# Moving the first three raw loads of w_out from ahead of V of chunk 1 to behind the reload of chunk 3's K, in a DeltaNet and MLP kernel

## The chip, the cores and the metric

The kernel runs on one core of a Trainium2 chip. The metric is the device time of one execution in microseconds (us). Three runs of the kernel before took 634.31, 634.44 and 635.64 us; their median is 634.44 us. Traces are stretched over one profiled execution, and their times count from its first instruction.

## The reference: what is computed

Two parts follow one another. The first is a DeltaNet recurrence for 4 batches of 8 heads, 768 tokens, 48 values per head:

```python
for t in range(S):
    kt, vt, bt = k_n[:, :, t], v[:, :, t], beta[:, :, t, None]
    y[:, :, t] = einsum('bhd,bhde->bhe', q[:, :, t], state)
    v_old = einsum('bhde,bhd->bhe', state, kt)
    state = state + bt[..., None] * einsum('bhd,bhe->bhde', kt, vt - v_old)
```

Here `k_n` is k divided by its norm. The second part is an MLP on the 3072 tokens of 384 values: `gelu(x @ w_in) @ w_out`, with `w_in` 384 x 2048 and `w_out` 2048 x 384. Both weights come in double precision, everything else in single precision.

## The kernel before, in words

**Tiling.** The 768 tokens are cut into 12 chunks of 64. One unit (`tiles[c, a]`) is chunk c of two batches, side by side on 128 partitions; every chunk has two units. For each chunk the kernel loads K, Q and V, forms products of K with itself and with Q, inverts a triangular system (an elimination of 32 rows on VectorE for the first two pairs of chunks, lines 503 to 529; on GpSimd later), solves for the updates, updates the state, and turns the result into tokens. The MLP of a chunk runs on TensorE beside the recurrence of the chunks that follow. From chunk 2 on, the MLP's products are formed by a scheme with fewer multiplications that needs sums of weights.

**The weights.** [...] There are 16 groups: 0 to 7 are `w_in`, 8 to 15 are `w_out`, two row blocks of `w_out` each. `fetch(n)` (line 206) issues the raw load of group n on SyncE: three DMAs of 256 KB for a group of `w_in`, into space that later holds `w_out` (the trace calls it `w_out_sb`), and two DMAs of 384 KB for a group of `w_out`, into one of three buffers `slots` (the trace calls them `w_raw`). The decoding of group n is `begin(n)` (VectorE, line 235 or 238), `exponents(n)` (ScalarE, line 241), `mantissas(n)` (VectorE, lines 255 and 257) and `signed(n)` (VectorE, line 264 for some groups, and 265). `signed(n)` then calls `fetch(n + 3)` for `w_out`, since its buffer is free: so groups 8, 9 and 10 are loaded by a loop of their own, and 11 to 15 by `signed(8)` to `signed(12)`.

**Order of the work.** The start, up to `by_hand.close()` (line 1260), is written out by hand for all engines. After it, `plan` lists steps with due times in units of a chunk; `emit` (line 1149) writes them in order of these times. In this second part VectorE keeps the written order, while a scheduler orders the other queues. SyncE issues nearly all DMAs, in order: an instruction that waits holds up all behind it. Eight completion semaphores serve its DMAs in turn, and each DMA first waits for the one eight places ahead to land.

**The lines around the change.** By hand, SyncE gets: Q of chunk 2 and K of chunk 3 (two units each), groups 2 and 3 of `w_in`, then groups 8, 9 and 10 of `w_out` (line 1205), then `load_v(1)`, V of chunk 1 (line 1207). V of chunk 1 is scaled on GpSimd (line 385), and read by VectorE in `subtract` (lines 738 and 744). In the plan follow the loads of groups 4 to 7 by `signed(0)` to `signed(3)`, then `load(3)` at 1.06 (line 1281; K and Q of chunk 3, K into its buffers once more), `load_v(2)` at 1.07 (line 1303; V of chunk 2), then the block-wise K of chunk 4 (`load_blocks`, line 138, 16 small DMAs into `Qp`). `begin(8)`, the first step that needs a raw group of `w_out`, is the first of `decode_steps(n_in, NW)`, at 1.365 and later (line 1279).

Of the kernel before, what the change touches and what calls it, by code (L numbers as in the profile page):

```python
# [19 lines left out]
def kernel(  # L20
# [122 lines left out]
    def load_v(c):  # L143
        if c >= NC:
            return
        for a in range(NA):
            u = tiles[c, a]
            u.V = io.tile([128, H, D], F32, tag="V", name="V", bufs=4)
            fetch_in(u.V, v, u)
# [47 lines left out]
    n_in = len(w_parts)  # L197
# [6 lines left out]
    slots = [su.tile([128, 2 * WG], U32, tag=f"w_raw{i}", name="w_raw", bufs=1) for i in range(3)]  # L204

    def fetch(n):
        if n >= len(w_parts):
            return
        dst, src = w_parts[n]
        if n < n_in:  # L210
            raw = stage[:, n % NS * 2 * WG:(n % NS + 1) * 2 * WG]
        else:
            raw = slots[(n - n_in) % len(slots)]
        w_raw[n] = raw.rearrange("q (n w) -> q n w", w=2)
        raw = raw.rearrange("q (m n w) -> q m n w", m=dst.shape[1], w=2)
        for m in range(dst.shape[1]):
            nc.sync.dma_start(out=raw[:, m], in_=src[:, m])
# [480 lines left out]
    def join_steps(g):  # L698
        a, b = range(NA), range(NA, 2 * NA)
        return [(join_run, g, a, ()), (join_run, g, b, a), (join_run, g, (), b)]  # L700
# [232 lines left out]
    def blocks(c):  # L933

        return FH // 2 if c < 4 else FH // 4
# [191 lines left out]
    def ffn_steps(c):  # L1127
        ones = [(1.3, fc1, c, f) for f in range(NF)]
        if c > 1:
            return [(0.88, part_of_layer, c, b, n) for b in range(FH // blocks(c))  # L1130
                    for n in ("P1", "P5", "P6", "P2", "R22", "R11", "P7", "P3", "R12", "P4", "R21")] + [
                (2.6, second_layer, cc, n) for cc in range(c, c + 1 + (c > 3))
                for n in (1, 5, 2, 6, 4, 7, 3)]
        twos = [(2.7, fc2, tiles[c, a], f, f + 4) for a in range(NA) for f in range(0, NF, 4)]
        if c == 0:
            twos.sort(key=lambda s: s[3])
            more_ = [(1.3, fc1, 1, f) for f in range(EARLY)]
            return ones + twos[:-2 * NA] + more_[:4] + twos[-2 * NA:-NA] + more_[4:] + twos[-NA:]
        return ones[EARLY:] + twos

    def at(first, last, steps):

        total, done, timed = sum(s[0] for s in steps), 0.0, []
        for w, *step in steps:
            timed.append((first + (last - first) * (done + 0.5 * w) / total, step))
            done += w
        return timed
# [54 lines left out]
        fetch_in(Qp[2 + a][:, :, 0:D], k, tiles[3, a])  # L1202
    for n in range(2, NS):
        fetch(n)
    for n in range(n_in, n_in + len(slots)):
        fetch(n)
    load_v(1)
    for u in third:
        transposed(u, (0,))
# [60 lines left out]
    def state_at(c, *times, first=(), second=(), last=()):  # L1270

        steps = state_steps(c, first, second, last)
        if len(times) > len(steps):
# [3 lines left out]
    plan = [at(c + 1 + 0.25 * (c == 1), c + 2 + 0.25 * (c == 0), ffn_steps(c)) for c in range(4)]  # L1277
    plan += [at(c + 1, c + 3, ffn_steps(c)) for c in range(4, NC, 2)]
    plan += [decode_in(), at(1.365, 1.9, decode_steps(n_in, NW)), at(1.91, 1.911, [(1.0, late)])]
    rows1, join1 = eliminate_steps(1), join_steps(1)  # L1280
    plan += [at(1.06, 1.065, [(1.0, load, 3)]),
             [(t, (join, 0, range(NA, 2 * NA), level)) for level, t in enumerate((1.085, 1.16))],
]
    sums = [(1.0, sum_of_squares, tiles[3, a], h) for a in range(NA) for h in range(H)]
# [63 lines left out]
    for c in (2, 3, *range(4, NC, 2)):  # L1348
        n = FH // blocks(c)
# [78 lines left out]
```

## Time and profile before

| what | value |
|---|---|
| median of three runs | 634.44 us (634.31 to 635.64) |
| span of the profiled execution | 633.5 us |
| median less span | 0.9 us |
| PE busy | 610.3 us, 96% of the span |
| VectorE (DVE) busy | 428.0 us, 68% |
| ScalarE (ACT) busy | 241.9 us, 38% |
| GpSimd (POOL) busy | 209.5 us, 33% |
| DMA, SyncE's queue | 37.34 MB, 30.7% of 16 engines' span |
| mean granted TensorE clock | 0.982 |
| raw loads of w_out, 16 DMAs of 384 KB | 3.3 to 8.1 us to landing, median 4.5 |

The profiled execution's own time is known by its span alone, 633.5 us from the first instruction to the last; what lies around it is taken as the 0.9 us by which the median of the runs is longer.

How to read it: "PE" is TensorE's matmuls, "PEld" its weight loads, "SPq" SyncE's instructions that issue DMAs. A line such as `L264` is line 264 of the kernel before. The chain of waits goes back from the last instruction, at each step to what released it. A busy share over the whole span is a mean over stages: up to about 137 us VectorE is the fullest engine or as full as TensorE, after that TensorE.

### The profile page before, as it was taken

To read this page: it belongs to the slowest core of one execution; us is meant where nothing else is said; L and a number is where in the kernel's file an instruction comes from. 1 tells how busy PE (TensorE), PEld (TensorE's weight loads), DVE (VectorE), ACT (ScalarE), POOL (GpSimd) and SP (SyncE) were. 2 spreads that over 40 slices of the span, in tenths; PEclk is the share of its full clock that TensorE was granted. 3 is DMA by queue.
4 is the path that set the end of the run, shared out by engine and by line. 5 is a ranking of instruction groups with operands and counts; after the bars stand their busy time and mean duration, and the time that the engine had idled before them with its cause. 6 is when DMAs were issued, how large, how long until landed. Compare 5 with 4: busy or idle time off the path is not lost.

```text
span 633.5 us, 20835 instructions
## 1 busy us (share of the span) xinstructions
PE 610.3 (96%) x8998; PEld 546.6 (86%) x8998; DVE 428.0 (68%) x783; ACT 241.9 (38%) x546; POOL 209.5 (33%) x316
## 2 busy tenths in 40 slices
PE   6769999999999989999999999999999999999997
PEld 5657786777899989998899998899998899988997
DVE  6999989999757586664867654968645955432532
ACT  3576877524541255224451124442034322034200
POOL 4044001000489521698112688112687100000000
PEclk9977999999999998999999999999999999999999
DMA  9894765102444423533123523024121001010011
GB/s 132 178 281 143 145 157 160 26 1 49 71 58 62 80 45 40 90 77 40 14 38 58 111 51 45 9 40 88 30 50 20 10 2 27 2 26 1 0 26 26
DMA packets 158428, 39.71 MB, mean 63 GB/s; under 512 B 150016, under 2 KB 153216, under 8 KB 158336
## 3 DMA queue, kind: packets, MB, share of 16 engines
q1 hardware_dynamic: 155664, 37.34, 30.7%
q10 hardware_dynamic: 2672, 1.03, 0.8%
q8 instruction: 71, 1.16, 0.8%
q14 instruction: 21, 0.17, 0.1%
HBM read 33.62 MB, written 4.72 MB: 61 GB/s over the span
## 4 chain that ended last, share of the span: by engine, by line
PE 77%; DVE 16%; issue 2%; SPq 2%; DMA 2%; ACT 1%; DVEq 0%
PE psX L928 12%; PE psY L994 10%; PE psY L928 8%; PE psX L994 8%; PE psV L994 5%; PE psZ L994 5%; PE psV L928 4%; PE psZ L928 4%; PE psK L727 3%; DVE tmp L523 3%; DVE Nu L525 3%; PE psO L895 3%; PE psG L423 2%; PE psH L877 2%; PE psY L792 2%
## 5 line engine op out<-in xcount | busy, mean ns | idle before, releaser
L360 POOL TENSOR_TENSOR n<-n,half 128x16 f32<-128x16 f32 x10 | 30.0, 3004 | 188.8 <-DVE n L358 139.0
L525 POOL TENSOR_TENSOR Nu<-Nu,tmp 128x30 f32<-128x30 f32 (+14 forms) x120 | 65.3, 544 | 9.0
L523 POOL TENSOR_TENSOR tmp<-Nu 128x30 f32<-128x30 f32 (+14 forms) x120 | 61.3, 510 | 9.3
L994 PE MATMUL psX<-xT,w_in_sb 128*128 128x256 f32 (+1 forms) x288 | 63.2, 350 | 0.0
L928 PE MATMUL psX<-w_out_sb,G 128*128 128x192 f32 x320 | 56.1, 329 | 0.0
L994 PEld LDWEIGHTS psX<-xT,w_in_sb 128*128 128x128 f32 x288 | 48.8, 194 | 5.1
L928 PEld LDWEIGHTS psX<-w_out_sb,G 128*128 128x128 f32 x320 | 52.2, 190 | 0.7
L877 PE MATMUL psH<-xT,w_in_sb 128*128 128x256 f32 x192 | 44.2, 384 | 1.6 <-ACT G L977 1.5
L895 PE MATMUL psO<-w_out_sb,G 128*128 128x384 f32 x128 | 43.9, 490 | 0.0
L877 PEld LDWEIGHTS psH<-xT,w_in_sb 128*128 128x128 f32 x192 | 35.7, 190 | 8.7 <-ACT G L977 2.5
L994 PE MATMUL psY<-xT,w_in_sb 128*128 128x256 f32 (+1 forms) x192 | 42.2, 350 | 0.0
L1022 DVE TENSOR_TENSOR psY<-psY,pu 128x512 f32<-128x512 f32 x20 | 14.0, 700 | 40.4 <-PE psY L994 38.9
L977 ACT COPY xT<-psX 128x768 f32<-128x768 f32 x9 | 7.2, 799 | 86.3 <-PE psX L854 86.3
L977 ACT COPY pu<-psZ 128x512 f32<-128x512 f32 x40 | 23.4, 586 | 37.3 <-PE psZ L994 37.3
L994 PEld LDWEIGHTS psY<-xT,w_in_sb 128*128 128x128 f32 x192 | 33.0, 197 | 3.3
L895 PEld LDWEIGHTS psO<-w_out_sb,G 128*128 128x128 f32 x128 | 23.6, 190 | 14.0
L977 ACT ACTIVATE G<-G 128x512 f32<-128x512 f32 x40 | 25.2, 630 | 19.5 <-DVE G L1030 19.4
L1030 DVE TENSOR_TENSOR G<-psY,pu 128x512 f32<-128x512 f32 x20 | 13.8, 689 | 23.4 <-PE psY L994 23.3
L928 PE MATMUL psZ<-T,pu 128*128 128x192 f32 x160 | 28.3, 329 | 0.1
L977 ACT ACTIVATE G<-psY 128x512 f32<-128x512 f32 x20 | 11.9, 597 | 42.7 <-PE psY L994 42.7
L928 PE MATMUL psY<-T,G 128*128 128x192 f32 x160 | 28.2, 329 | 0.0
L928 PE MATMUL psY<-w_out_sb,G 128*128 128x192 f32 x160 | 28.1, 329 | 0.0
(198 smaller groups left out, 1372.8 us busy)
## 6 DMA issues: line engine op xcount, KB each, us to landing
Kp<-in_k_dram SPq DMA_DIRECT2D x76, 96.0 KB, 3.3
w_out_sb<-in_moe_w_in_dram SPq DMA_DIRECT2D x24, 256.0 KB, 5.4
w_raw<-in_moe_w_out_dram SPq DMA_DIRECT2D x16, 384.0 KB, 4.5
V<-in_v_dram SPq DMA_DIRECT2D x48, 96.0 KB, 3.1
out_dram<-o_sb SPq DMA_DIRECT2D x40, 96.0 KB, 2.2
Qp<-in_k_dram SPq DMA_DIRECT2D x64, 32.0 KB, 2.1
Qp<-in_q_dram SPq DMA_DIRECT2D x64, 32.0 KB, 2.1
Qp<-in_q_dram SPq DMA_DIRECT2D x16, 96.0 KB, 4.3
```

The lines of the kernel that those rows point to most:

```text
L360: nc.gpsimd.tensor_tensor(flat, flat, half, op=ALU.pow)
L423: nc.tensor.matmul(psG[HALF[p], r, i * NP + j, :], lhsT=u.Kt[rows, p, j, :], rhs=(u.Qt if x else u.Kt)[rows, p, j, :], start=True, stop=True)
L523: rows_on.tensor_tensor(tmp, nu[:, j + 1:, j:j + 1].to_broadcast([128, n, j]), nu[:, j:j + 1, 0:j].to_broadcast([128, n, j]), op=ALU.mult)
L525: rows_on.tensor_tensor(nu[:, j + 1:, 0:j], nu[:, j + 1:, 0:j], tmp, op=ALU.add)
L727: nc.tensor.matmul(u.psK[to, x, r, j, :], lhsT=(u.Qt if x else u.Kt)[rows, p, j, :], rhs=St[rows, u.a, p ^ r, j, :], start=True, stop=True)
L877: nc.tensor.matmul(psH, lhsT=w_in_sb[:, f // 2, m, f % 2 * 128:(f % 2 + 1) * 128], rhs=xTs[c][:, m, :], start=(m == 0), stop=(m == NM - 1))
L895: nc.tensor.matmul(u.psO, lhsT=G[:, u.a, f, :], rhs=w_out_sb[:, f, :], start=(f == 0), stop=(f == NF - 1))
L928: nc.tensor.matmul(ps_, lhsT=lhs[:, f, :], rhs=rhs[:, f, :], start=first and f == 0, stop=f == FH - 1, skip_group_check=not first)
L977: i = fn(*args, **kw)
L994: nc.tensor.matmul(ps_[:, i], lhsT=lhs[:, f // 2, f % 2 * 128:(f % 2 + 1) * 128], rhs=rhs, start=first and i == 0, stop=True, skip_group_c ...
L1022: nc.vector.tensor_tensor(L1["Y1"], L1["Y1"], L1["pu"][:, 0], op=ALU.add)
L1030: nc.vector.tensor_tensor(half(1, 1), shaped(L1["Y1"]), shaped(L1["pu"][:, 0]), op=ALU.add)
```

## The change

The loop that loads groups 8, 9 and 10 leaves the part written by hand, where it stood ahead of `load_v(1)`, and becomes three steps of the plan, at 1.1 to 1.25:

```diff
     for n in range(2, NS):
-        fetch(n)
-    for n in range(n_in, n_in + len(slots)):
         fetch(n)
     load_v(1)
...
-    plan += [at(1.06, 1.065, [(1.0, load, 3)]),
+    plan += [at(1.06, 1.065, [(1.0, load, 3)]), at(1.1, 1.25, [(1.0, fetch, n) for n in range(n_in, n_in + len(slots))]),
```

In the order of the built programs, TensorE, VectorE and GpSimd keep all their instructions in the same order. On ScalarE four of the scalings of V of chunks 2 and 3 (line 382) change places with activations of `fc1` (line 883). On SyncE:

| place | before | after |
|---|---|---|
| behind group 3 of w_in | groups 8, 9, 10 (6 DMAs), V of chunk 1 | V of chunk 1 |
| next | groups 4 to 7 of w_in, K and Q of chunk 3, V of chunk 2 | the same |
| next | 16 small loads of K of chunk 4 | groups 8, 9, 10 (6 DMAs), then 5 of the 16 |
| next | group 11 | group 11, 10 of the 16 |
| next | 3 DMAs of another K of chunk 4, group 12 | group 12, the last of the 16 |
| next | V of chunk 3 among groups 13, 14 and 15, the last of that K | V of chunk 3 among groups 13, 14 and 15, then the 4 DMAs of that K |

From there on SyncE's order is the same in both.

## The prediction, made before the changed kernel ran

> **What bounds the kernel now.** The change touches loads between 33 and 104 us, so I first read the chain of waits over that stretch, then the timeline of SyncE's queue, then VectorE's timeline where the moved loads are consumed. The chain (start, length, engine and line):
>
> ```profile
> 82.78 2.79 PE psH L877 x12
> 85.56 0.61 PE psY L792 x32
> 86.17 0.47 PE psY L803 x32
> 86.64 0.47 PE psY L792 x32
> 87.11 0.51 PE psY L803 x31
> ...
> 87.64 0.55 DVE St L808
> 88.19 0.88 DVE w_e L264
> ...
> 135.54 2.05 DVE XM L534
> 137.58 0.14 issue
> 137.72 1.15 PE psJ L618 x32
> ```
>
> From 16 to 66 us the chain is VectorE's for the most part, from 66.04 to 87.62 TensorE's, from 87.64 to 137.6 VectorE's without a break, then TensorE's again. So a late raw group costs nothing before 87.64 as long as VectorE has slack, and its full lateness after. TensorE is no cushion there: its timeline has one idle gap from 92 to 140 us, 0.54 us before L618 at 137.72. SyncE's queue:
>
> ```profile
> 33.80 4.91 SPq L217 DMA_DIRECT2D w_raw<-in_moe_w_out_dram  x6
> 39.04 4.02 SPq L100 DMA_DIRECT2D V<-in_v_dram  x4
> 53.12 8.12 SPq L217 DMA_DIRECT2D w_out_sb<-in_moe_w_in_dram  x9
> ...
> 70.78 2.66 SPq L100 DMA_DIRECT2D V<-in_v_dram  x4
> 73.48 9.74 SPq L138 DMA_DIRECT2D Qp<-in_k_dram  x16
> 83.32 0.87 SPq L217 DMA_DIRECT2D w_raw<-in_moe_w_out_dram  x2
> ```
>
> The reader is to see that the six loads of groups 8 to 10 go out at 33.80 and that V of chunk 1 waits behind them. In the changed queue they follow V of chunk 2, so they start when its last issue ends, 73.4 us. Who needs them is in VectorE's timeline, `begin` of groups 8, 9 and 10 and the two steps behind:
>
> ```profile
> 79.21 0.55 DVE L238 TENSOR_SCALAR w_e<-w_raw 128x768 uint32<-128x768 uint32 x1
> ...
> 81.14 0.56 DVE L238 TENSOR_SCALAR w_e<-w_raw 128x768 uint32<-128x768 uint32 x1
> ...
> 84.94 0.55 DVE L238 TENSOR_SCALAR w_e<-w_raw 128x768 uint32<-128x768 uint32 x1
> 86.73 0.56 DVE L808 TENSOR_TENSOR St<-St,psY 128x384 f32<-128x384 f32 x1 [1.24 <-PE psY L803]
> ```
>
> The bracket is the slack: VectorE stands idle 1.24 us before 86.73, waiting for TensorE.
>
> **What leaves 33 to 48 us.** Six DMAs, 2.36 MB, and 4.91 us of SyncE's queue. V of chunk 1 is issued at about 33.8 instead of 39.04. Does anyone profit? (1) GpSimd scales this V at 49.25 (L385), right behind a memset that runs from 46.99 to 49.17; the four loads landed 7.1 to 7.7 us after their issues, and in the stretches of two us the DMA share is 0.29 from 45.8 to 47.8 and 0.03 after, so V was there before 49.25. The order on GpSimd is fixed and the memset waits for VectorE, so earlier V moves nothing. (2) VectorE itself could run faster with fewer DMAs beside it. The same 60 steps of the elimination run twice, once under this traffic. The view by stretches gives length, PE, PEld, DVE, ACT, POOL busy, clock, DMA share and GB/s:
>
> ```profile
> 16.18:39.04 22.86, 17.76 (x295) 14.87 (x296) 20.86 (x61) 14.48 (x53) 0.00 (x0) 0.97 0.87 214
> 112.57:135.44 22.87, 22.87 (x95) 17.59 (x94) 20.88 (x60) 9.39 (x34) 0.00 (x0) 1.00 0.07 18
> ```
>
> 22.86 us at a DMA share of 0.87, 22.87 at 0.07: traffic costs VectorE nothing. (3) No engine's wait from 30 to 46 us is for these loads. Gain: 0.
>
> **What arrives at 73 us.** The issues need eight places of older DMAs landed. K and Q of chunk 3, issued from 66.67 on with 3.5 to 4.5 us to landing, have landed; V's first two, issued near 70.8 and 71.4, land 4.0 later, by 75.4, in time for the fifth and sixth issue. At the 0.42 us of a median w_raw issue the six go out at 73.5, 73.9, 74.3, 74.8, 75.2 and 75.6. Landing: the later pairs of w_raw, behind a short queue, took 3.6 (at 83.3), 4.9 (at 89.1) and 5.4 us (at 92.9). The DMA share falls from 0.86 to 0.43 at 74.8, so V's backlog is short and I take this band: group 8's second DMA lands between 77.5 and 79.3. A DMA of 0.393 MB takes 0.98 us at the 402 GB/s of the sustained stretch; the first burst landed at steps of about 1.16 us (40.7 to 46.5 for six). Two more DMAs are 2.0 to 2.3 us: group 9 is there between 79.5 and 81.6, group 10 between 81.5 and 83.9. Needed: 79.21, 81.14, 84.94. So `begin(8)` is 0 to 0.1 us late, `begin(9)` 0 to 0.5.
>
> Cover for that: VectorE's 1.24 us. ScalarE holds a second one, since its L241 for group 9 (81.79) stands ahead of the activation that ends at 82.99 and frees the buffer that TensorE writes from 84.1 (the second six of the 12 L877 matmuls at 82.78): 1.1 us. Lateness of 0.5 is hidden; the cost is 0. If the cover is gone, each further us costs one.
>
> [...]
>
> **What stands behind in SyncE's queue.** Five small loads of chunk 4's K, then group 11. Group 11 waits for `signed(8)` (L264 ends at 82.56), so it goes out near 82.6 to 83.4, before 83.32. Then ten of the small loads at 0.45 to 0.61 us each (9.74 us for 16): 4.5 to 6.1 us, so group 12 goes out at 89.1 (its buffer is freed by VectorE at 89.06) to 90.2, before 89.14. It landed after 4.9 us, at about 94.4 for its second DMA, and is needed at 95.23: 0.8 us of cover against 0 to 1.1 us of delay, and the three K loads that competed with it before are gone. Cost 0, bound 0.3. Group 13 has the tighter cover, 93.3 + 5.4 = 98.7 against 99.03, but goes out when its buffer is free at 92.88 as before, with one V load issued ahead of it in both. Groups 14 and 15 likewise. V of chunk 3's last half and the other K of chunk 4 come at 100 to 104 us; ScalarE reads the one at about 115, the other at 148.5. The small loads are read by L408 at 151.87. Nothing there.
>
> ScalarE's exchange of four scalings of 0.25 us with activations, at 113 to 118 us, delays or hastens a TensorE buffer by 0.25 us; its cost lies between -0.1 and 0.2, and I take 0.
>
> **Sum.** 0 + 0 + 0 + 0: the span stays 633.5 us, and with the 0.9 us around it 634.4. I add 0.1 for the small waits at `begin(8)` and `begin(9)`: 634.5 us.
>
> **Rivals.**
>
> *Late groups, slower.* The first burst landed 6.9 to 8.1 us after issue. If the six land like that, since V's short rows clog the engines, group 8 is complete at 73.9 + 8.1 = 82.0, 2.8 us late. VectorE's 6.3 us of work from 79.21 then ends at 88.3, L808 slips by 1.55 and its second by 1.2; ScalarE's L241 for group 9 slips by 2.8, TensorE by 2.8 - 1.1 = 1.7. The end is 1.2 to 1.7 us later: 635.7 to 636.2. It decides from 1.1 us of lateness on. For it: one queue feeds the same 16 engines, and V takes a share of 0.67 to 0.86 at only 117 to 163 GB/s. Against it: at 33.8 six loads of 256 KB were queued ahead, at 73.4 only V's.
>
> *A late group 12 to 15, slower by less.* With 0.61 us for each small load and 4.9 us to landing, group 12 is up to 0.3 us late, and a pair of them 0.6: 634.8 to 635.1.
>
> *Earlier V helps, faster.* At 49.52 VectorE's L255 takes 1.19 us where others take 0.55, and L257 behind it 1.47 for 0.96, while GpSimd runs L385: 1.15 us on the chain. Were L385 held by V's landing, an earlier V would move it off these two: 634.4 - 1.15 = 633.3. Against it: GpSimd shows no wait before L385. [...] No run here shows it moved.
>
> *The change doesn't do what it says.* SyncE's queue as built does hold the six loads behind V of chunk 2, so this is excluded.
>
> **How the numbers follow.** No measurable change 0.68 (this holds 0.10 for the small late groups), late groups 0.22, faster 0.06; the rest, 0.04, is unnamed and I split it evenly. A measurement of this kernel can tell about 0.2%, 1.3 us, from no change. Late groups reach from 635.7 up, faster lies at 633.3 and below. Chances: faster 0.08, same 0.68, slower 0.24. The likeliest case alone spans 633.9 to 635.3. The range leaves out the faster case and the upper part of the slow one: 633.7 to 636.1.
>
> **What would show it.** Right: the six loads issue from 73.4, land by 84; L238 for groups 8 to 10 starts within 0.5 us of 79.2, 81.1 and 84.9; VectorE's idle time before L808 is shorter than 1.24 but above zero; L534 at 135.5. Wrong: a wait of VectorE for `w_raw` of over 1.1 us ahead of 86 us, or any wait for it from 88 to 108 us, which shifts L618 from 137.7 one for one; or L385 on GpSimd ahead of 49 us with L255 at 0.55 us.

## The result and the profile after

In one set of runs side by side the changed kernel took 636.31 us (median of 20, 632.70 to 637.87) and the kernel before 634.33 us (20, 632.54 to 637.22): a ratio of 1.0027, 95% interval 1.0015 to 1.0039. It is slower, by 2.0 us. Two later sets gave ratios of 0.9998 (0.9977 to 1.0019) and 1.0015 (0.9999 to 1.0031). All 43 runs of the changed kernel have a mean of 635.65 us, all 142 of the kernel before that this study holds 634.68: 0.97 us more, with twice the standard error at 0.5 (mine, from the listed times). Set by set the means differ by 1.8, 0.4 and 0.9 us. So it loses about 1 us, 0.15%; whether it is above or below the 0.2% that one set can tell is not settled. The two later sets ran on different chips, so a loss that differs from chip to chip isn't excluded.

The profiled execution has a span of 634.6 us (time 636.27). First the chain of waits (start, length, engine and line), the stretch that the prediction showed of before:

```profile
87.31 0.51 PE psY L803 x31
87.84 0.55 DVE St L808
...
92.19 0.88 DVE w_e L264
93.48 5.84 DMA w_raw<-in_moe_w_out_dram
99.41 0.57 DVE w_e L235
100.00 0.95 ACT w_e L241
...
138.26 1.15 PE psJ L618 x32
```

Before, VectorE carried this chain from 87.64 to 137.6 without a break. Now a raw load of `w_out` stands in it, 93.48 to 99.32, and VectorE's `begin(13)` behind it at 99.41 (before 99.03; half of these 0.38 us are there already at `begin(12)`, 95.44 against 95.23): group 13 has become the thing waited for, if by less than a bracket in the timeline shows. L618 comes at 138.26, 0.54 later than 137.72; the table below shows that the kernel before is as much later itself from one execution to the next. SyncE's queue:

```profile
34.33 4.47 SPq L100 DMA_DIRECT2D V<-in_v_dram  x4
...
70.44 2.67 SPq L100 DMA_DIRECT2D V<-in_v_dram  x4
73.15 3.90 SPq L217 DMA_DIRECT2D w_raw<-in_moe_w_out_dram  x6
77.09 3.93 SPq L138 DMA_DIRECT2D Qp<-in_k_dram  x5
83.43 0.82 SPq L217 DMA_DIRECT2D w_raw<-in_moe_w_out_dram  x2
84.31 5.88 SPq L138 DMA_DIRECT2D Qp<-in_k_dram  x10
90.28 0.87 SPq L217 DMA_DIRECT2D w_raw<-in_moe_w_out_dram  x2
```

V of chunk 1 goes out at 34.33 and the six loads of groups 8 to 10 at 73.15, as forecast. The last two lines are the ten small loads and then group 12, at 90.28; before it went at 89.14. Between the five small loads and group 11 the queue stands idle from 81.02 to 83.43. VectorE's `begin(8)` and `begin(9)`, and the step that waits for TensorE:

```profile
79.40 0.55 DVE L238 TENSOR_SCALAR w_e<-w_raw 128x768 uint32<-128x768 uint32 x1
81.97 0.56 DVE L238 TENSOR_SCALAR w_e<-w_raw 128x768 uint32<-128x768 uint32 x1 [0.56 <-DMA w_raw<-in_moe_w_out_dram]
86.91 0.55 DVE L808 TENSOR_TENSOR St<-St,psY 128x384 f32<-128x384 f32 x1 [0.58 <-PE psY L803]
```

The bracket in the second line is new: VectorE stands idle 0.56 us for group 9. The third line shows where it went: the 1.24 us of idle time before L808 has shrunk to 0.58, and L808 itself is 0.18 late. So far this is the forecast.

### The profile page after: what moved, and what is told of

Its sections match the earlier page's. It is cut to its first block, busy times and chain, and to the rows that moved or that the text cites. A ratio compares the mean times of both kernels' runs of the same rounds, so it can differ in the third digit from the quotient of the medians.

```text
span 634.6 us, 20837 instructions
## 1 busy us (share of the span) xinstructions
PE 611.7 (96%) x8998; PEld 547.4 (86%) x8998; DVE 428.5 (68%) x783; ACT 241.7 (38%) x546; POOL 209.8 (33%) x316
## 4 chain that ended last, share of the span: by engine, by line
PE 78%; DVE 11%; ACT 3%; SPq 3%; issue 2%; DMA 2%; DVEq 0%
PE psX L928 12%; PE psY L994 10%; PE psY L928 8%; PE psX L994 7%; PE psV L994 5%; PE psZ L994 5%; PE psG L423 4%; PE psV L928 4%; PE psZ L928 4%; PE psK L727 3%; PE psO L895 3%; SPq L138 2%; PE psH L877 2%; PE psY L792 2%; PE psU L762 2%
## 5 line engine op out<-in xcount | busy, mean ns | idle before, releaser
L877 PE MATMUL psH<-xT,w_in_sb 128*128 128x256 f32 x192 | 45.5, 393 | 0.3
```

The source lines that it names most:

```text
L877: nc.tensor.matmul(psH, lhsT=w_in_sb[:, f // 2, m, f % 2 * 128:(f % 2 + 1) * 128], rhs=xTs[c][:, m, :], start=(m == 0), stop=(m == NM - 1))
```

## The experiments

**Theories.** A: the loss is VectorE's waits for raw groups of `w_out` between 79 and 110 us. B: it is chance, from TensorE's clock and gaps behind 110 us. C: it comes from the front, from V of chunk 1 going ahead at 34 us or from TensorE's granted clock, which was 0.50 from 38.56 to 59.04 us in the trace of the changed kernel and for 13.65 us between 37.59 and 54.66 in that of before. All runs below are to be read with the table behind them (in edited kernels the decoding lines move: `begin` is L237 and L240 in some, L808 is L810). It gives, for one profiled execution of each kernel, how much later than in the first profile of before VectorE's same instruction starts (its order is the same in all): L534 at 39.14, L307 at 109.33, L408 at 238.14, L808 at 251.28. Beside it stand the waits of VectorE for raw groups of `w_out` that its timeline shows in brackets, added up; how long TensorE's granted clock was 0.50 near 236 us; and the span, all in us.

### The two kernels again

No edit: the kernel before, and the changed kernel.

> The kernel before, unchanged, as a control and for a second profile. Theory A (waits of VectorE for raw groups of w_out between 81 and 106 us make the loss), theory B (the loss is chance: TensorE's half-clock periods and issue gaps after 110 us, which differ from execution to execution), theory C (the loss comes from the front: V of chunk 1 ahead, and TensorE at half clock from 38.6 to 59.1 us): all three give 0.998 to 1.002. Its profile tells which of the differences between the first two traces repeat: A expects no wait of VectorE for w_raw and L307 at 109.3 us, C expects TensorE at half clock for some 13 us of the stretch from 37 to 60.

> The changed kernel once more. A and C: 1.002 to 1.004 again (1.2 to 2.5 us). B: 1.000 to 1.001. In the profile A expects VectorE's L238 for group 9 near 82.0 with a wait of some 0.5 us, L235 for group 13 at 99.3 or later, and L307 at 109.8, 0.5 us behind the kernel before; C expects TensorE at half clock for 20 us between 38 and 60 us.

Measured: `before_again` 634.87 us, ratio 1.0004 (0.9985 to 1.0024); `after_again` 634.09, ratio 0.9998 (0.9977 to 1.0019), but its profiled execution took 640.01 with a span of 638.3. VectorE's timeline of `after_again` shows what one execution can lose:

```profile
83.96 0.56 DVE L238 TENSOR_SCALAR w_e<-w_raw 128x768 uint32<-128x768 uint32 x1 [1.72 <-DMA w_raw<-in_moe_w_out_dram]
88.58 0.56 DVE L808 TENSOR_TENSOR St<-St,psY 128x384 f32<-128x384 f32 x1 [0.27 <-PE psY L803]
...
98.10 0.56 DVE L235 TENSOR_SCALAR w_e<-w_raw 128x768 int32<-128x768 int32 x1 [0.90 <-DMA w_raw<-in_moe_w_out_dram]
109.77 0.56 DVE L238 TENSOR_SCALAR w_e<-w_raw 128x768 uint32<-128x768 uint32 x1 [2.19 <-DMA w_raw<-in_moe_w_out_dram]
```

Groups 9, 12 and 15 are waited for, 5.2 us in all with group 8; the cover before L808 is nearly used up (0.27), and L307 is 5.1 us late. The place speaks for A, the size varies from one execution to the next. The ratio alone does not: 0.9998 lies outside the 1.002 to 1.004 that A expected and near what B expected, and L307 is ten times as late as A's 0.5 us.

### The small loads out of the way

`kb_last`: the changed kernel, with the 16 small loads of chunk 4's K issued behind group 15. The core of the edit; the rest notes which instruction issued each group, and moves the due time of the small loads from 1.8 to 2.05:

```diff
+    def blocks_behind(*args):
+        with tc.issue_after(fetched[NW - 1]):
+            load_blocks(*args)
-            plan += [at(t, t + 0.01, [(1.0, load_blocks, c, name, src)])]
+            plan += [at(t, t + 0.01, [(1.0, blocks_behind if (c, name) == (4, "Kb") else load_blocks, c, name, src)])]
```

> The changed kernel with the 16 small loads of K of chunk 4 moved behind groups 11 to 15 and behind V of chunk 3, so that groups 11 to 13 meet no small loads in SyncE's queue. A, if the price is paid at groups 12 and 13: 0.999 to 1.001, and L307 back at 109.3 to 109.5. A, if it is paid at group 9: 1.002 to 1.003. B: 1.000 to 1.001. C: 1.002 to 1.004.

Measured: 635.64 us, ratio 1.0014 (0.9997 to 1.0031). VectorE waits 2.4 us for groups 8, 9 and 14, and L307 is 2.0 us late. So the small loads in the queue are not what makes groups 8 and 9 late, and group 14 can be late without them. The ratio lies between A's two bands and decides nothing; L307 was to be back at 109.3 to 109.5 if the price were paid at groups 12 and 13, and it is not.

### The groups ahead of V of chunk 2

`mid`: the changed kernel, the six loads issued ahead of V of chunk 2 instead of behind it, at 71.1. The core of the edit; the last two lines stand in a step of their own that issues V of chunk 2:

```diff
-             at(1.1, 1.25, [(1.0, fetch, n) for n in range(n_in, n_in + len(slots))]),
+             at(1.065, 1.069, [(1.0, fetch, n) for n in range(n_in, n_in + len(slots))]),
+        with tc.issue_after(fetched[n_in + len(slots) - 1]):
+            load_v(c)
```

> The changed kernel with groups 8 to 10 issued one place earlier, between K and Q of chunk 3 and V of chunk 2, 2.7 us sooner; what follows stays. A, if the price is paid at group 9: 0.999 to 1.001 and no wait before L238 for group 9. A, if it is paid at groups 12 and 13: 1.001 to 1.003, since their queue is the same. B: 1.000 to 1.001. C: 1.002 to 1.004.

Measured: 636.04 us, ratio 1.0017 (0.9999 to 1.0036). VectorE's timeline:

```profile
96.76 0.56 DVE L237 TENSOR_SCALAR w_e<-w_raw 128x768 int32<-128x768 int32 x1 [1.36 <-DMA w_raw<-in_moe_w_out_dram]
...
102.18 0.56 DVE L237 TENSOR_SCALAR w_e<-w_raw 128x768 int32<-128x768 int32 x1 [1.54 <-DMA w_raw<-in_moe_w_out_dram]
```

No wait at groups 8 to 10 any more (the first L808 keeps 1.22 us of idle time), and yet 2.9 us at groups 12 and 13, and L307 3.2 us late. These are groups that the change does not touch. Their loads go out late. Five of the small loads took SyncE 5.10 us (79.51 to 84.61) instead of some 3 us (five of sixteen that took 9.74), so group 11 went out at 84.70, 2.0 us after its buffer was free at 82.65. Ten more took 6.14 us, and group 12 went out at 91.86 (before 89.14). This is A with the price at groups 12 and 13, for which 1.001 to 1.003 was expected, though the interval just holds 1.

### The early half alone

`v1_first`, run twice (`v1_again`): the kernel before, V of chunk 1 ahead of the three groups.

```diff
+    load_v(1)
     for n in range(n_in, n_in + len(slots)):
         fetch(n)
-    load_v(1)
```

> The kernel before with one edit: V of chunk 1 is issued ahead of groups 8 to 10 of w_out instead of behind them, so the early half of the change alone; the groups still come 30 us before they are needed. Theory A (the loss is VectorE waiting for raw groups of w_out between 79 and 110 us): no wait of VectorE for w_raw, its step L307 within 0.3 us of 109.3, the time that of before, 634.4, within 0.8. Theory C (the changed order at 34 to 45 us costs, by TensorE's clock or by other traffic): L534 near 39 to 59 us or the end is later by 1.5 us or more, 636.

> V of chunk 1 ahead of the early groups, a second time: its first ratio was 0.9989 (0.9975 to 1.0004). Theory A: no waits for w_raw, L307 at 109 to 110.2, ratio 1 within 0.2%, and not faster than before. The rival that an earlier V of chunk 1 is a gain: ratio again 0.997 to 0.999.

Measured: 634.38 us, ratio 0.9989 (0.9975 to 1.0004), and 635.42, ratio 1.0008 (0.9991 to 1.0024). No wait in one profile, 0.64 us at group 14 in the other. A's expectations of L307 missed both times: 110.00 against 109.3 within 0.3, and 110.75 against 109 to 110.2, the second with a wait where none was expected. The front brings no gain and costs nothing that two sets can tell, and L534 is no later than in the profiles of before (+0.16 and +0.52 against up to +0.61); C falls.

### The later queue alone

`tail_only`: the kernel before, groups 8 to 10 early, but the small loads cut in 5, 10 and 1 around groups 11 and 12 as in the changed queue. The core of the edit; the rest cuts the small loads into pieces:

```diff
-            fetch(after)
+            if after in (n_in + 3, n_in + 4):
+                with tc.issue_after(blocks4[-1]):
+                    fetch(after)
+                piece(*((5, 15), (15, 16))[after - n_in - 3], after)
+            else:
+                fetch(after)
```

> The kernel before with groups 8 to 10 of w_out early, but with the 16 small loads of chunk 4's K cut in 5, 10 and 1 around groups 11 and 12, as they stand in the changed kernel's queue; so the late half alone, without the six big loads beside it. If the loss comes from the later place of groups 12 and 13 in the queue: VectorE waits for w_raw at groups 12 to 15, 0.3 to 2 us in all, L307 at 109.6 to 111.3, time 634.8 to 636.4. If it comes from the six loads themselves and what they push back: no such wait, 634.4 within 0.8. Theory B (only chance of TensorE's clock): 634.4.

Measured: 635.08 us, ratio 1.0003 (0.9988 to 1.0018); one wait, 0.28 us at group 14. Here the first five small loads take SyncE 2.61 us; behind the six big loads they took 3.93, 5.33 and 3.44 in the three profiles of the changed kernel. Group 12 goes out at 90.21, about as late as in the changed kernel (90.28), and is not waited for. So in this profile the new order of the later queue alone makes no waits larger than the kernel before has by itself (up to 1.1 us, below). It isn't excluded as a part of the price: 635.08 and L307 at 110.26 lie inside the bands for it, and the interval reaches up to 0.18%.

### Larger doses

`late5` and `late16`: the changed kernel, the six loads behind 5 or behind all 16 of the small loads. The core of the edit in `late5`, where `blocks4` holds the five loads issued so far and the other eleven follow the groups; in `late16` it holds all sixteen:

```diff
+        with tc.issue_after(blocks4[-1]):
+            fetch(n_in)
+        for n in range(n_in + 1, n_in + len(slots)):
+            fetch(n)
```

> The changed kernel with groups 8 to 10 issued behind five of the small loads of chunk 4's K, so about 2.4 us later than in it (75.8 instead of 73.4), and the other eleven small loads behind them. Theory A, dose: group 8 lands 2 to 3 us later than in the changed kernel's runs, so VectorE's shift at L307 is 2 to 3 us above theirs (0.5 and 5.1 us seen): 3 to 7 us; of this 0 to 2.6 us are given back at 236 to 251 us; time 636 to 640. Theory B: no dose, 634 to 636.4 as for the changed kernel.

> The changed kernel with groups 8 to 10 issued behind all 16 small loads of chunk 4's K, about 9.7 us later than in it (83 instead of 73.4). Theory A, large dose: group 8's second load lands at 87 to 90 instead of 79, VectorE has 1.2 us of cover and some steps behind, so L307 is later than before by 7 to 10 us, and the time 640 to 644 (up to 2.6 us given back at 236 to 251 us). Theory B: no dose, 634 to 636.4.

Measured: 638.70 us, ratio 1.0069 (1.0047 to 1.0090), with 4.7 us of waits; and 642.87 us (6 runs), ratio 1.0127 (1.0106 to 1.0147), with 10.2 us. From `late16`'s VectorE timeline, `begin(8)` and `begin(9)`:

```profile
88.61 0.56 DVE L240 TENSOR_SCALAR w_e<-w_raw 128x768 uint32<-128x768 uint32 x1 [8.98 <-DMA w_raw<-in_moe_w_out_dram]
91.51 0.56 DVE L240 TENSOR_SCALAR w_e<-w_raw 128x768 uint32<-128x768 uint32 x1 [0.89 <-DMA w_raw<-in_moe_w_out_dram]
```

The six loads go out at 84.06 in `late16`, 10.9 later than at 73.15; L307 is 9.8 us late and the end 6.9 us. `late5` has L307 5.4 us late. All four numbers lie in A's bands; B, which knows no dose, falls as the cause of the loss. In `late16` none of the 16 small loads stands between groups 10 and 12, and all but 0.33 us of the waits are at groups 8 and 9: the late groups themselves are paid for there.

### One group of the three

`one_late`: groups 8 and 9 early, behind V of chunk 1, only group 10 behind V of chunk 2.

```diff
+    for n in range(n_in, n_in + 2):
+        fetch(n)
-             at(1.1, 1.25, [(1.0, fetch, n) for n in range(n_in, n_in + len(slots))]),
+             at(1.1, 1.25, [(1.0, fetch, n_in + 2)]),
```

> A third of the move: groups 8 and 9 of w_out early, behind V of chunk 1, and only group 10, which is needed at 84.9, behind V of chunk 2 at about 73.3. Theory A: group 10 lands by 79, no wait for it; what follows in the queue comes later by two issues, 1.3 us at most, of which the gaps before groups 11 to 13 take some; so no wait at groups 8 to 10, 0 to 0.5 us at groups 12 to 15, L307 at 109.0 to 110.3, time 634 to 635.2. A rival, that any big load between V of chunk 2 and the small loads sets off the loss: VectorE waits over 1 us for w_raw, time 635.5 to 636.5.

Measured: 634.16 us, ratio 0.9996 (0.9983 to 1.0009), no wait at all. Two big loads in that place cost nothing that can be told, six do; the rival that any would do it falls. The queue behind differs too (twelve small loads ahead of group 11 and four behind it), so the number of loads is not all that changed.

### The two kernels a third time

> The changed kernel a third time, for one more profile and twelve more times. Two profiles of it showed 0.6 and 5.2 us of VectorE's waits for w_raw, and two sets of times 636.3 and 634.1. Theory A: waits again, between 0.5 and 6 us in all, L307 at 109.8 to 115, time 634.5 to 637. Theory B (chance after 110 us): L307 at 109.3, time 634.4.

> The kernel before a third time. Theory A: no wait of VectorE for w_raw, or under 0.3 us, L307 at 109 to 110, as in its two profiles so far; ratio 1 within 0.2%. Theory B: waits of several us here too.

Measured: `after_third` 635.69 us, ratio 1.0015 (0.9999 to 1.0031), waits of 0.9 us at groups 9 and 15. `before_third` 635.19 us, ratio 1.0008 (0.9994 to 1.0023), and here I had expected under 0.3 us of waits: it has 1.1 us, at groups 13, 14 and 15, and L307 at 111.64 instead of 109 to 110. The longest wait is this one:

```profile
103.81 0.56 DVE L235 TENSOR_SCALAR w_e<-w_raw 128x768 int32<-128x768 int32 x1 [0.67 <-DMA w_raw<-in_moe_w_out_dram]
```

Groups 13 to 15 have no sure reserve already in the kernel before.

### All profiles

| kernel | waits for w_raw | L534, 39.14 | L307, 109.33 | L408, 238.14 | half clock near 236 | L808, 251.28 | span |
|---|---|---|---|---|---|---|---|
| before | 0 | 0 | 0 | 0 | 6.8 | 0 | 633.5 |
| before_again | 0 | -0.19 | +0.14 | +0.43 | 6.8 | +0.43 | 634.0 |
| before_third | 1.1 | +0.61 | +2.31 | +1.83 | none | -0.72 | 632.7 |
| v1_first | 0 | +0.16 | +0.67 | +1.00 | 3.4 | -0.48 | 633.2 |
| v1_again | 0.6 | +0.52 | +1.42 | +1.49 | 3.4 | +0.36 | 633.9 |
| tail_only | 0.3 | +0.42 | +0.93 | +0.94 | 3.4 | -0.53 | 633.4 |
| one_late | 0 | +0.96 | +0.98 | +1.27 | 3.4 | -0.09 | 633.5 |
| after | 0.6 | -0.13 | +0.50 | +0.81 | 3.4 | -0.73 | 634.6 |
| after_again | 5.2 | +0.35 | +5.11 | +5.67 | 3.4 | +4.47 | 638.3 |
| after_third | 0.9 | +0.98 | +1.56 | +1.68 | 3.4 | +0.56 | 634.4 |
| kb_last | 2.4 | +0.27 | +1.99 | +1.51 | none | -1.05 | 632.5 |
| mid | 2.9 | +0.10 | +3.18 | +3.23 | none | +0.67 | 634.4 |
| late5 | 4.7 | +0.85 | +5.40 | +5.45 | none | +2.89 | 636.6 |
| late16 | 10.2 | +0.36 | +9.84 | +9.49 | none | +6.94 | 640.4 |

Two things are in it. From 39 to 109 us the seven profiles with the groups early (down to `one_late`) grow by 0.57 us on average, the three of the changed kernel by 0.63, 4.76 and 0.58, so 1.99: 1.4 us more, against 1.0 +- 0.5 in the times. Three profiles are few for that mean, and one of them makes it: the other two grow no more than the early ones do. With `kb_last` and `mid`, which issue the six loads at 74.9 and 71.1, the mean of five is 2.15. From 109 to 238 us, where ScalarE's exchange lies, the three profiles of the changed kernel grow by 0.31, 0.56 and 0.12, those of before by 0, 0.29 and -0.48: no cost of the exchange near 1 us is seen. And from 238 to 251 us every profile makes one of three steps: 0 where TensorE ran 6.8 us at half clock, -1.1 to -1.5 where 3.4, -2.55 where none. The step goes by these periods and not by the lateness: `before_third` makes the same one as `late16`. So 2.6 us of any difference between two single traces can be that draw. The first trace of before holds the dearest draw and that of after a middle one, which hides 1.5 us; after's span is longer all the same, because a gap of 1.15 us on TensorE ahead of L727 near 412 us stands in it alone. Why it does is open.

## Why the prediction was right or wrong

The forecast was 634.5 us and no measurable change; the first set gave 636.31 us, 0.2 above the top of the range, and all sets together 635.65, inside it and 1.15 above the forecast. The mechanism that the text named as a danger, late groups, is the one that acts. The step that failed is the landing of group 9, and what hangs on it in the queue. Point by point:

- **"What leaves 33 to 48 us": gain 0.** Right within what the sets can tell: 0.9989 and 1.0008 for `v1_first` and `v1_again`. The rival of a faster kernel by an earlier V did not occur: in `v1_first` V of chunk 1 goes out at 34.84, and L385 on GpSimd still starts right behind the memset, at 49.76, with L255 still at 1.19 us beside it.
- **"What arrives at 73 us".** The issue time was right (73.15 against about 73.4). The landing was too early: group 9 was to be there between 79.5 and 81.6, and VectorE got it at 81.97, 83.96 and 82.68 in the three profiles, 0.4 to 2.4 us past the upper end. The term that failed is "two more DMAs are 2.0 to 2.3 us". From the landing of group 8's second DMA to that of group 9's it took 3.44 us (78.44 to 81.88), 3.74 and 2.56. The view by stretches of the changed kernel (length, PE, PEld, DVE, ACT, POOL busy, clock, DMA share, GB/s):

```profile
76.00:78.00 2.00, 2.00 (x43) 1.79 (x36) 1.97 (x4) 1.70 (x3) 0.00 (x0) 1.00 0.97 370
78.00:80.00 2.00, 2.00 (x11) 1.75 (x10) 2.00 (x5) 0.87 (x4) 0.00 (x0) 1.00 0.95 291
80.00:82.00 2.00, 2.00 (x20) 1.50 (x20) 1.41 (x3) 1.20 (x2) 0.00 (x0) 1.00 1.01 387
```

  The engines are full (share 0.95 to 1.01) at a mean of 349 GB/s, below the 402 of the forecast. At that rate a DMA takes 1.13 us and two take 2.25, still inside the 2.0 to 2.3: the rate alone does not make the 3.44 us. Between the two landings the view gives 342 GB/s, so the engines moved some 1.18 MB, an estimate, where two DMAs are 0.79 MB. At most 0.13 MB of the rest can be the five small loads, so at least some 0.25 MB were of group 10: the loads moved in part side by side, where the forecast let each land behind the one ahead. `kb_last` has 3.29 us there without a small load. The 402 GB/s of the forecast is not reached here, though the kernel before reached it elsewhere (403 GB/s from 39 to 41 us, 410 from 41 to 43).
- **"Cover for that".** Right: lateness of 0.56 and 0.43 us vanished in the idle time before L808 (1.24 to 0.58 and 0.69). In `after_again` the 2.1 us of waits at groups 8 and 9 took 0.97 from that idle time (0.27 left of 1.24) and pushed L808 by the other 1.1: the cover is about what the text put it at.
- **"What stands behind in SyncE's queue": cost 0, bound 0.3.** The waits at groups 12 to 15 are 0, 3.1 and 0.5 us in the three profiles. The ten small loads took 5.88, 5.76 and 5.81 us, inside the 4.5 to 6.1 of the text. What failed is "it goes out near 82.6 to 83.4" for group 11: it went at 83.43, 85.42 and 84.14. In the first of these traces the load eight places ahead of it, group 9's second, landed at 81.88, and SyncE's wait for that ended at 81.90; `signed(8)` came last, its L264 ending at 83.40. Group 11 waits for `signed(8)`, which stands behind `begin(9)` on VectorE, so a late group 9 makes the whole queue behind it late. In `after_again` VectorE's 2.1 us of waits at groups 8 and 9 came ahead of `signed(8)`; group 11 and then the ten small loads followed, and group 12 went out at 92.14, 1.2 us after its buffer was free at 90.94. VectorE waited 0.9 us for it, and 2.19 us for group 15, whose second load took 7.3 us to landing (5.2 and 5.6 in the other two profiles); why it did is open. The five small loads ahead of group 11 were longer too, 3.4 to 5.3 us instead of 2.6; in the first trace of the changed kernel the second and the fourth took 0.89 and 1.25 us to issue, where 0.45 is common. Each of the five started 0.36 us or more after the load eight places ahead had landed, so what lengthened them is not shown. But the queue then stood idle for 2.3 to 2.4 us before group 11 in all three profiles, so in the changed kernel they delayed nothing. In `mid` they did. "Group 13 ... goes out when its buffer is free at 92.88 as before": it went at 93.09, 94.76 and 93.91, with VectorE itself later.
- **The covers as constants.** The text set landing times of one trace against needs of the same trace. The three profiles of before have 0, 0 and 1.1 us of waits at groups 13 to 15: the 0.3 us of cover found for group 13 is smaller than what the landing times vary by. A cost of "0, bound 0.3" could not be had from it.
- **"0.9 us around it".** No run shows this term. Every listed time is 1.7 to 1.9 us above its own span, so the execution that the forecast was read from took about 635.2 us, an estimate, 0.8 more than the median. The sum is the median of the kernel before by the way the 0.9 was made, so the forecast is not shifted by it.
- **The signs.** The first trace shows neither sign of being wrong, though `begin(9)` and `begin(10)` miss the 0.5 us of the signs of being right (81.97 and 85.78). `after_again` shows both (1.72 us at group 9, then groups 12 and 15), `after_third` the second (0.49 us at 106.23).
- **The rivals.** "Late groups, slower" priced 635.7 to 636.2; "a late group 12 to 15" 634.8 to 635.1. Both happen, and in `after_again` together: the first set's median lies 0.1 above the first, the mean of all runs between the two. They were priced apart and not added, though the same six loads cause both and the first brings on the second.

That late groups cost time through VectorE's waits is shown by dose (`late5`, `late16`), and kernels with the groups early (`v1_first`, `one_late`) show no loss. That the changed kernel's own 1 us is made of these waits fits, but rests on three profiles, of which one holds nearly all of it. How its waits are spread over executions, and how much of them falls to groups 8 and 9 and how much to the queue behind, stays open. A fourth buffer for the raw groups, which would let group 12 go out earlier, was not tried.

## What to carry to other kernels

A load that is moved later is not paid for at its own consumer alone: look at the later loads that wait for a buffer which this consumer frees, at what stands between them in the queue, and at whether the issues of loads behind take longer beside the ones moved ahead of them (five small loads took SyncE 5.10 us in `mid`, 2.61 in `tail_only`). A load that is issued together with others need not land as if those behind it were not there: here 3.44 us lay between the landings of groups 8 and 9, with some 1.18 MB moved, an estimate, where the two DMAs of group 9 are 0.79 MB. Cover found in one trace counts only as far as it exceeds what landing times vary by from one execution to the next; take that from a second profile, or from the spread of the same load's landings. Where single traces are compared, find first what differs in steps (here the clock periods), or a gain of 1.5 us by chance hides the loss that is looked for.

## What the runs showed of the hardware

**In the first traces of before and of the changed kernel the changes of TensorE's granted clock lie multiples of 3.413 us apart.** Before, it changes at 37.59, 41.00, 44.42, 54.66, 235.56 and 242.39 us; between these lie 3.413, 3.413, 10.240, 180.906 and 6.827 us, that is 1, 1, 3, 53 and 2 times 3.413. In the changed kernel it changes at 38.56, 59.04, 236.53 and 239.95 us, with 20.480, 177.493 and 3.413 us between, 6, 52 and 1 times 3.413; 236.53 is 0.97 later than 235.56, so the two traces don't share these times. Near 236 us TensorE has a gap ahead of L727, 1.4 to 2.0 us in the six timelines that show it. Stretches of 3.41 us, first of the kernel before, on both sides of its change at 235.56, then of `mid`, where the clock stays at 1.00 and the place of the cuts is the author's estimate (columns as above):

```profile
232.15:235.56 3.41, 1.98 (x113) 1.75 (x112) 2.00 (x4) 1.57 (x3) 0.00 (x0) 1.00 0.02 5
235.56:238.97 3.41, 3.00 (x28) 2.91 (x28) 2.24 (x5) 0.76 (x2) 0.00 (x0) 0.50 0.03 7
```

```profile
235.21:238.63 3.42, 2.54 (x119) 2.30 (x118) 2.21 (x4) 1.69 (x3) 0.00 (x0) 1.00 0.03 7
238.63:242.04 3.41, 2.61 (x36) 2.56 (x37) 2.08 (x5) 1.18 (x3) 0.00 (x0) 1.00 0.02 5
```

Before: 1.3 us of a gap of 1.7 lie in the first stretch, TensorE is busy 1.98 of 3.41 us there, 58%, and the next stretch has a clock of 0.50. `mid`: the cut divides the gap into 0.9 and 0.8 us, both stretches are busy for over 2.5 us, and the clock stays at 1.00. Near 236 us the emptiest stretch of the 14 profiles was followed by half clock in nine, where TensorE was busy for 1.46 to 2.00 us, and not in five, where it was busy for 2.00 to 2.54 (busy with modelled ends; the cuts of these five are the author's estimate). The rest of the kernel doesn't go by this: in the trace of before, the stretch from 61.48 us with 1.90 us busy at full clock was followed by full clock, and the one from 47.83, busy throughout at half clock, by half clock again. What decides is open. Between the profiles this draw makes a difference of up to 2.55 us, while single times of the kernel before lie between 632 and 638 us.
